# The v of an attention batch's ninth block in a tile of its own

## The chip, the cores and the metric

One core of a Trainium2 chip runs the whole kernel. The metric is the device time of one execution in microseconds (us), the median of three runs. A profile of one further execution shows what each engine did: PE is TensorE (the matrix engine, PEld its weight loads), DVE is VectorE, ACT is ScalarE, POOL is GpSimd, and SP is SyncE, which here only issues DMAs. SPq is SP's queue of such issues.

## The reference, cut to what matters

Inputs `q`, `k`, `v` have shape (4 batches, 8 heads, 576 positions, 64). Three blocks follow one another:

```python
# 1. attention with a window of 64
scores = q @ k.T / 8, masked to 0 <= pos_q - pos_k < 64
attn = softmax(scores)
x = (attn @ v)            # -> (4, 576, 512) after the heads are joined
# 2. Fourier mixing and an MLP
u = x + real(fft over positions and channels)
x = u + relu(layernorm(u) @ w_ch1) @ w_ch2      # 512 -> 2048 -> 512
# 3. a spatially gated MLP
h = gelu(x @ w_in); u, v = halves of h
out = x + (u * (w_sg @ layernorm(v) + b_sg)) @ w_out
```

The change touches only the loading of the attention's `v`.

## The kernel before

Each batch of 576 positions is cut into nine blocks of 64 (`NB = 9`), so attention walks over 36 blocks, numbered n = 9b + j. A block's keys and values are the 128 positions that end with its own 64. For each block the function `attention` does `scores(n)` (eight TensorE matmuls on L328, then on VectorE the masked minimum on L333, then on ScalarE the exponential on L335), `transposes(n)` (L342, copied out by ScalarE on L344), and then, for two blocks at a time, `pv` (L355: 32 products of 65 columns, written to the PSUM tile `pv`, of which there is one buffer). The ninth block, j = 8, has no partner: its `pv` has 16 products. `norm` divides by the row sums on VectorE (L370, L371 and L374); its last instruction, L374, is the last reader of the PSUM tile. `xt` transposes the result (L384), and the folds on L464 to L474 begin the Fourier stage.

The loop runs over steps n = 0 to 38. In step n it emits scores(n), then `load_attn(n + 4)`, then transposes(n - 1), then pv(n - 2) where a pair or a ninth block is complete, then xt(n - 3). `drive` puts pieces of other work between these: the Fourier stage and layernorm of finished batches, and the decoding of weights, which loads 256 KB pieces (`dec_s`, L162) through the same SP queue.

What is loaded when: `load_q` brings q for two blocks in two DMAs (L284, a ring of `QB = 3` tiles), `load_k` brings k for three blocks (L273, three buffers), `load_v` brings v for two blocks in one DMA of 520 KB (L301), and for the ninth block in one of 260 KB (L296). All of v goes through one ring of `VB = 3` tiles of 2 x 520 floats per partition; the ninth block takes a whole one of these and fills half of it. With `VL = 2`, the load for block (b, j) is emitted in step 9b + j - 2, and the pair's pv in step 9b + j + 3.

The order on each engine is not the order of the program text. The kernel is built with `schedule_with_timeline_sim=True` (L1529): at build time a planner simulates the engines and picks, on each engine, the next instruction among those that are ready in the simulation, by priority, which without further marks is the order in which they were emitted. That order is then fixed; each engine works through its list and waits where something is missing. A load into a ring tile is ready when the tile's last reader is done.

Of the kernel before, what the change touches and what calls it, by code (L numbers as in the profile page):

```python
# [11 lines left out]
F32 = mybir.dt.float32  # L12
# [9 lines left out]
NB = S // 64  # L22
# [91 lines left out]
class Kernel:  # L114
# [172 lines left out]

    def load_v(self, b, j):

        w = min(2, NB - j)  # L290
        t = self.ap_.tile([128, 2, 520], F32, tag="v", bufs=VB, name="v")
        v = self.aps["v"][b]
        for i in range(w):
            self.vt[b, j + i] = t[:, i]
        if w == 1:
            self.nc.sync.dma_start(t[:, 0], v[64 * j:64 * j + 128, :])  # L296
        else:
            src = v[64 * j:64 * j + 128, :]
            ap = [list(x) for x in src.ap]
            src = bass.AP(tensor=src.tensor, offset=src.offset, ap=[ap[0], [64 * 520, 2], ap[1]])  # L300
            self.nc.sync.dma_start(t, src)  # L301

    def load_attn(self, n):
        if n < B * NB:
            b, j = divmod(n, NB)
            if n < 2:
                self.load_q(b, j, 1)
            elif j % 2 == 0:
                self.load_q(b, j, min(2, NB - j))
            if j % 3 == 0:  # L310
                self.load_k(b, j // 3)
        if VL <= n < B * NB + VL:
            b, j = divmod(n - VL, NB)
            if j % 2 == 0:
                self.load_v(b, j)

    def attention(self):
# [1218 lines left out]
```

## Time and profile before

| what | value |
|---|---|
| median of 3 runs | 765.17 us (764.11 to 766.25) |
| the profiled execution: its own time | 765.43 us |
| the profiled execution: span from first to last instruction | 763.6 us, mean granted TensorE clock 0.998 |
| TensorE busy | 746.0 us of the span |
| v loads | 16 of 520 KB, 4 of 260 KB |

The span is 1.83 us shorter than the profiled execution's own time. [...]

### The profile page before, as it was taken

The numbers are of one execution on the slowest core, as the hardware profiler recorded it, in microseconds if no ns is written. First come the engines' busy times: TensorE is split into PE (matmuls) and PEld (weight loads), VectorE is DVE, ScalarE is ACT, GpSimd is POOL, SyncE is SP. The second block draws the span as 40 slices with busy tenths as digits, with TensorE's granted clock in tenths as the row PEclk, the third lists the DMA queues.
The fourth block names the chain that finished last, engine by engine and source line by source line (L and its number), as shares of the span: only waits on it lengthen the run. The fifth ranks groups of instructions, "written<-read, shape, count | busy, mean of one in ns | idle before, by whom it ended". The sixth has DMA issues, their size and how long they took to land.

```text
span 763.6 us, 13934 instructions
## 1 busy us (share of the span) xinstructions
PE 746.0 (98%) x4994; PEld 720.1 (94%) x4994; DVE 526.7 (69%) x1482; ACT 350.9 (46%) x837; POOL 192.6 (25%) x244
## 2 busy tenths in 40 slices
PE   7999899899999999999999999999999999999998
PEld 6798798899999999999999999999999898999897
DVE  4768857983446599874588658546987679674662
ACT  5896996745144566331245224124646454231220
POOL 2344464434214450065321112021102211010100
PEclk9999999999999999999999999999999999999999
DMA  9998761433016888584838914753111141114023
GB/s 267 320 298 258 202 209 43 140 110 125 1 30 215 281 262 292 190 330 161 319 118 318 355 59 151 289 207 124 57 58 32 40 132 33 63 32 135 11 73 124
DMA packets 84773, 123.37 MB, mean 162 GB/s; under 512 B 24416, under 2 KB 61664, under 8 KB 84704
## 3 DMA queue, kind: packets, MB, share of 16 engines
q1 hardware_dynamic: 82912, 119.13, 47.0%
q0 software_dynamic: 576, 2.97, 1.0%
q8 instruction: 39, 0.64, 0.3%
q10 hardware_dynamic: 1216, 0.39, 0.2%
q14 instruction: 30, 0.25, 0.1%
HBM read 91.79 MB, written 30.67 MB: 160 GB/s over the span
## 4 chain that ended last, share of the span: by engine, by line
PE 77%; DVE 3%; DMA 1%; issue 1%; ACT 0%; ACTq 0%
PE w L130 7%; PE w L132 7%; PE w L131 7%; PE c L132 6%; PE c L131 6%; PE c L130 6%; PE g L130 6%; PE g L132 6%; PE g L131 5%; PE acc L131 3%; PE acc L132 3%; PE h L130 3%; PE h L131 3%; PE h L132 3%; PE acc L130 3%; DMA dec_s<-in_wo 1%
## 5 line engine op out<-in xcount | busy, mean ns | idle before, releaser
L171 ACT ACTIVATE set<-dec_w 128x256 fp32r<-128x256 f32 x111 | 45.0, 414 | 68.8 <-PE w L131 31.1
L846 POOL TENSOR_TENSOR u<-u 128x384 f32<-128x384 f32 x15 | 18.6, 1243 | 184.8 <-ACT u L845 126.4
L619 POOL TENSOR_TENSOR rq<-rq,mhalf 128x1 f32<-128x1 f32 (+1 forms) x24 | 16.0, 665 | 150.8 <-DVE rq L618 149.7
L335 ACT ACTIVATE s<-s,mx 128x128 f32<-128x128 f32 x144 | 47.5, 393 | 13.3 <-DVE mx L333 13.2
L172 DVE TENSOR_TENSOR set<-dec_w,set 128x256 fp32r<-128x256 f32 x99 | 45.4, 467 | 9.7 <-ACT set L171 3.6
L333 DVE CUSTOM_DVE_ANT_0 s<-sc,mask 128x128 f32<-128x128 f32 x144 | 33.3, 284 | 24.7 <-PE sc L328 13.2
L165 ACT ACTIVATE dec_g<-dec_s 128x256 f32<-128x256 f32 x88 | 37.5, 428 | 27.4 <-DMA dec_s<-in_wi 11.5
L132 PE MATMUL acc<-rh,set 128*128 128x384 f32 x144 | 48.6, 338 | 0.0
L131 PE MATMUL acc<-rl,set 128*128 128x384 f32 x144 | 48.5, 337 | 0.0
L130 PE MATMUL acc<-rh,set 128*128 128x384 f32 x144 | 46.7, 337 | 0.0
L167 DVE SCALAR_TENSOR_TENSOR dec_w<-dec_g,dec_w 128x256 int32<-128x256 int32 x88 | 42.0, 480 | 3.2 <-ACT dec_g L165 2.9
L328 PE MATMUL sc<-k,q 128*128 128x128 f32 x288 | 40.2, 287 | 3.2 <-DVE mx L333 1.8
L846 DVE TENSOR_TENSOR u<-w,u 128x384 f32<-128x384 f32 x44 | 24.3, 552 | 27.4 <-POOL u L846 22.6
L328 PEld LDWEIGHTS sc<-k,q 128*128 128x128 f32 x288 | 35.8, 197 | 5.1 <-issue 1.8
L893 DVE TENSOR_TENSOR uT<-g,uT 128x384 f32<-128x384 f32 x36 | 19.3, 553 | 28.1 <-PE g L132 28.1
L130 PE MATMUL c<-set,set 128*128 128x320 f32 (+2 forms) x120 | 36.2, 303 | 0.0
L132 PE MATMUL c<-set,set 128*128 128x320 f32 (+2 forms) x120 | 36.0, 303 | 0.0
L718 DVE SCALAR_TENSOR_TENSOR rl<-h,rh 128x384 fp32r<-128x384 f32 x36 | 19.8, 551 | 23.3 <-ACT rh L717 23.3
L131 PE MATMUL c<-set,set 128*128 128x320 f32 (+2 forms) x117 | 35.1, 302 | 0.0
L166 DVE TENSOR_SCALAR dec_w<-dec_s 128x256 int32<-128x256 int32 x88 | 31.0, 361 | 5.0 <-DMA dec_s<-in_wo 3.5
L355 PEld LDWEIGHTS pv<-v,pts 128*64 128x64 f32 x576 | 23.3, 139 | 8.0 <-issue 6.4
L845 ACT ACTIVATE u<-w 128x384 f32<-128x384 f32 x29 | 14.1, 487 | 35.9 <-PE w L132 35.0
(383 smaller groups left out, 2603.2 us busy)
## 6 DMA issues: line engine op xcount, KB each, us to landing
dec_s<-in_w SPq DMA_DIRECT2D x64, 256.0 KB, 3.2
v<-in_v SPq DMA_DIRECT2D x16, 520.0 KB, 5.1
xht<-xb SPq DMA_DIRECT2D x10, 768.0 KB, 8.3
xhm<-xb SPq DMA_DIRECT2D x10, 768.0 KB, 7.6
xlm<-xb SPq DMA_DIRECT2D x8, 768.0 KB, 8.2
k<-in_k SPq DMA_DIRECT2D x11, 512.0 KB, 6.3
xf<-u SPq DMA_DIRECT2D x18, 256.0 KB, 3.1
p<-xf SPq DMA_DIRECT2D x24, 192.0 KB, 3.8
```

The source lines that it names most:

```text
L130: mm(out, lhsT=lh, rhs=rh, start=first and i == 0, stop=False)
L131: mm(out, lhsT=lh, rhs=rl, start=False, stop=False)
L132: mm(out, lhsT=ll, rhs=rh, start=False, stop=last and i == n - 1)
L165: nc.scalar.activation(out=g, in_=s[:, :, 1].bitcast(F32), func=AF.Prelu, scale=2.0 ** -112, alpha=-2.0 ** 32)
L166: nc.vector.tensor_scalar(out=w, in0=s[:, :, 0], scalar1=29, scalar2=None, op0=ALU.logical_shift_right)
L167: nc.vector.scalar_tensor_tensor(out=w, in0=g[:].bitcast(I32), scalar=3, in1=w, op0=ALU.logical_shift_left, op1=ALU.bitwise_or)
L171: self.nc.scalar.activation(out=hi, in_=f, func=AF.Copy)
L172: self.low.tensor_tensor(out=lo, in0=f, in1=hi, op=ALU.subtract)
L328: nc.tensor.matmul(sc[:, hp], lhsT=q[:, hp].rearrange("p a b -> p (a b)"), rhs=k[:, hp, o:o + 128], start=True, stop=True)
L333: nc.vector.tensor_tensor_reduce(out=s[:, hp], in0=sc[:, hp], in1=mask, scale=-0.125, scalar=1e30, op0=ALU.add, op1=ALU.min, accum_out=mx[ ...
L335: nc.scalar.activation(out=s[:, hp], in_=s[:, hp], func=AF.Exp, bias=mx[:, hp:hp + 1], scale=-1.0)
L846: add = lambda eng, o, i, j: eng.tensor_tensor(out=o, in0=i, in1=j, op=ALU.add)
```

## The change

The ninth block's v gets a tile of its own under the tag `vlast` (520 floats per partition, one buffer). It is fetched right behind the pair of blocks 6 and 7, in the same call of `load_v`. So its load moves from step 9b + 6 to step 9b + 4 of the loop. The ring of three tiles holds pairs alone: four tiles a batch pass through it instead of five. The number of DMAs, their sizes and sources stay as they were, as do all matmuls. The attention's memory pool grows by 2,080 bytes per partition.

```diff
     def load_v(self, b, j):
-        w = min(2, NB - j)
         t = self.ap_.tile([128, 2, 520], F32, tag="v", bufs=VB, name="v")
         v = self.aps["v"][b]
-        for i in range(w):
+        for i in range(2):
             self.vt[b, j + i] = t[:, i]
-        if w == 1:
-            self.nc.sync.dma_start(t[:, 0], v[64 * j:64 * j + 128, :])
-        else:
-            src = v[64 * j:64 * j + 128, :]
-            ap = [list(x) for x in src.ap]
-            src = bass.AP(tensor=src.tensor, offset=src.offset, ap=[ap[0], [64 * 520, 2], ap[1]])
-            self.nc.sync.dma_start(t, src)
+        src = v[64 * j:64 * j + 128, :]
+        ap = [list(x) for x in src.ap]
+        src = bass.AP(tensor=src.tensor, offset=src.offset, ap=[ap[0], [64 * 520, 2], ap[1]])
+        self.nc.sync.dma_start(t, src)
+        if j == NB - 3:
+            last = self.vt[b, NB - 1] = self.ap_.tile([128, 520], F32, tag="vlast", name="vlast")
+            self.nc.sync.dma_start(last, v[64 * NB - 64:64 * NB + 64, :])
 ...
-            if j % 2 == 0:
+            if j % 2 == 0 and j < NB - 1:
                 self.load_v(b, j)
```

## Rows read from the trace of the kernel before

**Rows 1.** The page: busy us, share of the span and instructions of each engine.
```profile
PE 746.0 (98%) x4994; PEld 720.1 (94%) x4994; DVE 526.7 (69%) x1482; ACT 350.9 (46%) x837; POOL 192.6 (25%) x244
```

**Rows 2.** TensorE's waits over the whole span: us in total, times, longest.
```profile
PE pv L355 <- issue: 2.1, 1, 2.1
...
PE sc L328 <- DMA k<-in_k: 1.3, 2, 1.2
```

**Rows 3.** Windows: length, busy us of each engine, PEclk, DMA share, GB/s.
```profile
20.00:40.00 20.00, 18.47 (x218) 16.08 (x217) 15.73 (x90) 16.50 (x47) 7.52 (x15) 1.00 1.04 327
40.00:60.00 20.00, 19.70 (x227) 18.05 (x227) 13.58 (x78) 18.25 (x58) 8.75 (x17) 1.00 0.97 289
60.00:80.00 20.00, 19.36 (x210) 17.88 (x209) 18.11 (x80) 14.06 (x41) 8.97 (x14) 1.00 0.86 249
80.00:100.00 20.00, 17.14 (x193) 15.31 (x192) 15.46 (x74) 19.44 (x51) 9.32 (x15) 0.91 0.68 184
100.00:120.00 20.00, 20.00 (x233) 18.17 (x231) 12.65 (x69) 17.79 (x51) 13.05 (x19) 1.00 0.56 179
...
140.00:763.60 623.60, 616.64 (x3637) 603.64 (x3637) 426.34 (x1004) 241.71 (x543) 131.66 (x134) 1.00 0.43 148
```

**Rows 4.** Waits of SP's own queue, 60 to 120 us.
```profile
SPq L301 <- PE pv L355: 12.8, 7, 2.8
SPq L506 <- DVE uT L568: 10.2, 2, 10.0
SPq L296 <- PE pv L355: 7.7, 1, 7.7
```

**Rows 5.** Timeline of SP's queue, 17 to 35 us: start, us, issue.
```profile
17.26 0.38 SPq L301 DMA_DIRECT2D v<-in_v  x1
17.84 2.90 SPq L284 DMA_DIRECT2D q<-in_q  x2
...
22.82 1.18 SPq L296 DMA_DIRECT2D v<-in_v  x1
24.10 5.24 SPq L284 DMA_DIRECT2D q<-in_q  x4
...
32.90 0.57 SPq L301 DMA_DIRECT2D v<-in_v  x1
...
34.55 0.44 SPq L301 DMA_DIRECT2D v<-in_v  x1
```

**Rows 6.** Issue to landing: q issued at 20.1, two q from 24.1, v at 34.55.
```profile
DMA to landing us min/median/max: 8.2/8.2/8.2
...
DMA to landing us min/median/max: 9.1/9.3/9.5
...
DMA to landing us min/median/max: 9.7/9.7/9.7
```

**Rows 7.** Timeline of TensorE, 30 to 46 us.
```profile
30.50 2.05 PE L328 MATMUL sc<-k,q 128*128 128x128 f32 x16
...
34.57 1.95 PE L328 MATMUL sc<-k,q 128*128 128x128 f32 x16
...
40.59 1.15 PE L355 MATMUL pv<-v,pts 128*64 128x65 f32 x32
...
44.54 0.33 PE L355 MATMUL pv<-v,pts 128*64 128x65 f32 x2
```

**Rows 8.** Timeline of TensorE around 85 us, with the idle time before.
```profile
85.23 0.30 PE L355 MATMUL pv<-v,pts 128*64 128x65 f32 x2 [2.09 <-issue]
```

**Rows 9.** Timeline of VectorE, 82 to 85 us.
```profile
82.06 1.16 DVE L166 TENSOR_SCALAR dec_w<-dec_s 128x256 int32<-128x256 int32 x1
...
84.45 0.68 DVE L374 TENSOR_TENSOR x<-pv,rd 128x512 f32<-128x512 f32 x1
```

**Rows 10.** Window behind that wait, columns as in Rows 3.
```profile
86.00:88.00 2.00, 2.00 (x11) 1.92 (x10) 1.61 (x7) 1.88 (x7) 1.08 (x3) 0.50 0.49 167
```

**Rows 11.** Groups by line on VectorE, 17 to 108 us: busy us, mean ns.
```profile
L166 DVE TENSOR_SCALAR dec_w<-dec_s 128x256 int32<-128x256 int32 x12 | 4.9, 431 | 0.0
```

## The prediction

> **What bounds the kernel now.** I read first the busy shares, then TensorE's waits, then the windows of the attention stage, then the queue on which v is loaded, and last the few microseconds where TensorE does stand still. TensorE is busy for 746.0 of 763.6 us [rows 1]; the reader is to see that only 17.6 us of idleness exist in the whole kernel. The change touches the attention, which ends near 130 us. From 140 us on TensorE is idle for 623.6 - 616.6 = 7.0 us in 624 [rows 3], and nothing of v is left there. Between 20 and 120 us, where the changed loads lie, the windows give idleness of 1.53, 0.30, 0.64, 2.86 and 0.00 us, together 5.3 us. The window from 80 to 100 us also has a mean granted clock of 0.91: 20 x 0.09 = 1.8 us of full-speed work are lost there. So what the change can win by straightening this stage is at most 5.3 + 1.8 = 7.1 us, 0.9% of the time, and only if it removes every stall there.
>
> Does TensorE wait for v? The list of its waits has only one DMA, k, with 1.3 us, and no v [rows 2]. Its longest wait in the stretch is put down to "issue", 2.1 us before a pv [rows 2, 8]. The code says what that is: pv's PSUM tile has one buffer, and its last reader on VectorE, L374, ran from 84.45 to 85.13; the pv started at 85.23 [rows 8, 9]. That wait is for VectorE, not for v.
>
> Who does wait for v's ring is SP: seven v pairs waited 12.8 us and one ninth block 7.7 us for a pv to free a ring tile [rows 4]. This is the wait that the change attacks. It is a wait of a queue that runs ahead of the engines.
>
> **The change part by part.** *The ring.* Before, a load waits for the reader of the third load before it, and every fifth load is a ninth block. After, the ninth blocks don't count. Batch b+1's first three pairs then wait for batch b's pairs 2, 4 and 6 in place of 4, 6 and the ninth, so each may go one pv earlier; the fourth waits for the first, as before. Queued behind a waiting v load are q, k and weight pieces, and TensorE waits for none of these after the start [rows 2]. I cost the shorter waits at 0: their cover is that v is early already. Where it is least early, v issued at 34.55 lands after 9.7 us, at 44.25, and its pv starts at 44.54 [rows 5 to 7]: 0.3 us to spare, which grows when this load goes earlier. So a gain by landing alone is not to be had, as no pv waits for one.
>
> *The ninth block's load* moves in the first batch from 22.82 to right behind the pair at 17.26, past the two q loads at 17.84 [rows 5]. Its 260 KB at the 327 GB/s that this stretch reached [rows 3] are 0.8 us more in front of those q loads. The second of them starts no later than 20.74 and lands 8.2 us later [rows 5, 6], at 28.9 at most; TensorE needs it for the scores at 30.50 [rows 7]. 28.9 + 0.8 = 29.7: hidden, with 0.8 us left. That slack is the cover; without it the price is 0.8 us once. In the later batches DMA is less full (shares 0.86, 0.68 and 0.56 against 1.04) [rows 3], so I take 0 there too. [...]
>
> *The first pair of the second batch* becomes ready earlier: it needs the pv of the first batch's pair 2 and not pair 4. It was issued at 32.90, behind four q and a k [rows 5]. It can now come before the four q at 24.10, or behind the first two of them. Bound above: 520 KB at 327 GB/s are 1.6 us. The first q pair from 24.10 lands after 9.1 to 9.5 us, at some 33.8; the scores that need it start at 34.57 [rows 5 to 7], 0.8 us later. So a v put in front costs TensorE up to 1.6 - 0.8 = 0.8 us, and one put behind costs nothing. In the order of emission the q pair comes first, so I take 0 and keep 0.8 for the range.
>
> *The order on TensorE.* The planner sees v earlier, so it may put a pv earlier. The pv of the second batch's first pair is emitted in step 12 of the loop, but ran at 40.59, behind the scores of blocks 13 and 14 [rows 7] (scores come in eights, and the two sixteens there are blocks 9 to 12). A pv placed earlier gives TensorE work in its small holes; all idleness from 20 to 60 us is 1.83 us [rows 3], which bounds this gain from above, and 0 from below. I take 0.4, about a fifth, since the holes I can name there come from VectorE and ScalarE too.
>
> *Sum.* Ring 0, ninth block 0, q order 0, pv order -0.4: the profiled execution's 765.43 us become 765.0. That execution lies 0.26 above the median of the three runs, so for a median I say **764.8 us**, the same as before within 0.3% (2.3 us, about what a measurement of this kernel can tell from no change).
>
> **The rivals.** What speaks against "no change" is that the order on all engines is made at build time from simulated times, and v's readiness is one of its inputs. A pv moved by one place moves VectorE's and ScalarE's lists too. [...]
>
> *Faster: the stall at 83 us goes.* Ring waits of up to 2.8 us lie on SP in the same stretch [rows 4], so the lists around it will be remade. L374 came late because VectorE first did weight decoding (L166, 1.16 us where the mean is 0.43) and three masked minima [rows 9, 11]. If L374 comes first, or the pv behind other TensorE work, 3.9 us are won: 765.17 - 3.9 = 761.3. With the small holes before it (1.8 + 0.6 us) it ends near 759; the bound is 765.17 - 7.1 = 758.1. For it speaks that the change only loosens: no load is ready later than before. Against it: nothing in the stall is v.
>
> *Slower: one more stall of this kind.* Its place is the single pv buffer between L374 and the next pv, in any of 20 pv's. If the planner draws a pv forward, because its v is there, to where VectorE still has decoding and folds ahead of the previous L374, TensorE, which can't pass it, stands. It decides from 2.3 us of idleness, or from 0.5 us if the clock falls as it did at 83 us. A stall like the seen one gives 765.17 + 3.9 = 769.1; with the q load of 0.8 us on top 769.9. [...]
>
> *The change does not do what it says.* If the planner keeps its order, SP only waits less and every engine list stays; the time is 765.2. That falls within "no change".
>
> **How the numbers follow.** No change within 0.3%: 0.42, and it is the likeliest single case, so its sum is the predicted time; its own range is 763 to 767.4. Faster, by a stall removed: 0.34. Slower, by a stall made: 0.24; less than faster because readiness is only loosened. The range goes down to 760.0 (the 83 us stall gone and about 1.3 us of the small holes) and up to 769.5 (one new stall of 3.9 us, with half of the q price), which leaves about 1 in 10 outside on either side.
>
> **What would show it.** Right: on SP, waits of L301 for pv fall from 12.8 us to under half, and the last ninth block no longer waits 7.7 us; its load stands directly behind the fourth pair of its batch; TensorE's busy time stays within 1 us of 746.0, and its waits still name no v. The scores at 30.50 and 34.57 start no later than before relative to the pv in front of them. Wrong: the window 80 to 100 us with a clock of 1.00 and under 1 us of idleness (the faster rival), or another window of the attention with a clock below 0.95 or a new pv wait over 2 us (the slower one). My working fails as a whole if the time moves by more than 2.3 us and the idle time between 20 and 140 us does not account for it: then the order behind 140 us was changed too, which I hold for unlikely.

## The result, and the profile after

The changed kernel takes 769.84 us (median of 7 runs, 768.05 to 773.59); the kernel before takes 765.17 (7 runs). The ratio is 1.006, with a 95% interval of 1.0043 to 1.0076: slower by 0.6%, some 4.7 us, where no change was forecast. The profiled execution has a span of 766.6 us, 3.0 us more than the one before; single executions of one kernel lie up to 3.8 us (before) and 5.5 us (changed) apart, so a trace shows where time goes better than how much in the median.

The place of the loss is plain. Number TensorE's matmuls from 0 and count time from the start of the first, which lies at 2.14 us of the span in both traces. Matmul 120 then starts at the same time in both (17.02 and 17.05 us), matmul 300 starts 3.98 us later than before (36.03 against 32.05), matmul 1,320 starts 3.23 us later and the last one 2.90 us later. So all of it is lost between 19 and 38 us of the span, around the end of the first batch, and nothing is lost after the attention. The windows of the changed kernel (columns as in Rows 3; PEclk is the granted TensorE clock as a share of full speed, the DMA share the mean busy share of the 16 DMA engines):

```profile
20.00:40.00 20.00, 16.60 (x189) 14.25 (x187) 13.18 (x68) 12.98 (x35) 4.54 (x13) 0.91 1.14 293
...
28.00:32.00 4.00, 1.65 (x11) 1.19 (x10) 1.68 (x6) 1.80 (x5) 1.65 (x3) 0.94 1.18 295
32.00:36.00 4.00, 4.00 (x45) 3.55 (x44) 2.45 (x8) 0.88 (x2) 0.50 (x2) 0.63 1.17 282
...
80.00:100.00 20.00, 16.37 (x193) 14.33 (x194) 16.93 (x90) 19.15 (x51) 8.47 (x13) 1.00 0.91 227
```

Against [rows 3], the window from 20 to 40 us has 1.9 us more idleness and a granted clock of 0.91 in place of 1.00, another 1.8 us. The clock fell behind the idleness: TensorE was busy for 1.65 of the 4 us from 28 to 32, and the next 4 us were granted 0.63. The window from 80 to 100 us, where the clock had been 0.91, now has 1.00. Note the last two columns: the DMA engines are busier than before (1.14 against 1.04), and move less (293 against 327 GB/s).

TensorE's timeline there, with the wait that was foretold not to come:

```profile
29.18 0.44 PE L383 MATMUL xt<-ident,x 128*128 128x128 f32 x2 [0.99 <-DVE x L373]
30.98 0.30 PE L354 MATMUL pv<-v,pts 128*64 128x65 f32 x2 [1.36 <-DMA v<-in_v]
...
34.32 2.35 PE L327 MATMUL sc<-k,q 128*128 128x128 f32 x16
```

The pv of the first batch's fourth pair waits 1.36 us for its v, and the scores of blocks 9 and 10 start at 34.32, where they had started at 30.50 [rows 7]. SP's queue ahead of it (start, us, issue):

```profile
14.88 0.60 SPq L300 DMA_DIRECT2D vlast<-in_v  x1
15.53 0.56 SPq L273 DMA_DIRECT2D k<-in_k  x1
16.14 2.18 SPq L162 DMA_DIRECT2D dec_s<-in_w  x2
18.41 0.38 SPq L297 DMA_DIRECT2D v<-in_v  x1
22.43 1.73 SPq L284 DMA_DIRECT2D q<-in_q  x2
...
25.20 1.32 SPq L297 DMA_DIRECT2D v<-in_v  x1
26.62 2.49 SPq L284 DMA_DIRECT2D q<-in_q  x1
```

The first ninth block was not put behind its pair, as the text of the change has it: it waits for no ring tile, so the planner found it ready sooner and put it ahead of a k, two weight pieces and the pair itself. In the other three batches, too, the ninth block's load was issued ahead of its pair (42.01 against 51.86 us in the second). The pair, issued at 18.41 (17.26 before, [rows 5]), took this long to land:

```profile
DMA to landing us min/median/max: 12.4/12.4/12.4
```

It reads like a case of order: 260 KB pushed in front of a pair that was then late. The experiments say otherwise.

What the change was for did happen. SP's waits for pv between 60 and 120 us, 12.8 and 7.7 us in [rows 4], are now:

```profile
SPq L297 <- PE pv L354: 5.8, 2, 3.7
...
SPq L300 <- PE pv L354: 2.9, 2, 2.1
```

Part of that fall is not the change's own. In the changed kernel with q back in its old place (e1 and e9 below, the same order) these waits are 9.0 and 5.5 us in one trace and 5.2 and 5.2 us in the other: the sum falls from 20.5 us to 14.5 and 10.4, and to 8.7 where q's loads are slow.

### The profile page after: what moved, and what is told of

It reads as the page before. It is cut to its first block, busy times and chain, and to the rows that moved or that the text cites. A ratio compares the mean times of both kernels' runs of the same rounds, so it can differ in the third digit from the quotient of the medians.

```text
span 766.6 us, 13933 instructions
## 1 busy us (share of the span) xinstructions
PE 747.5 (98%) x4994; PEld 720.5 (94%) x4994; DVE 528.1 (69%) x1482; ACT 351.6 (46%) x837; POOL 191.1 (25%) x244
## 4 chain that ended last, share of the span: by engine, by line
PE 82%; DVE 5%; DMA 2%; issue 1%; ACT 1%; ACTq 0%; DVEq 0%
PE w L130 7%; PE w L132 7%; PE w L131 7%; PE c L132 6%; PE g L130 6%; PE c L131 6%; PE c L130 6%; PE g L132 6%; PE g L131 6%; PE acc L131 3%; PE acc L132 3%; PE h L130 3%; PE h L132 3%; PE acc L130 3%; PE h L131 3%; PE pv L354 1%
## 5 line engine op out<-in xcount | busy, mean ns | idle before, releaser
L332 DVE CUSTOM_DVE_ANT_0 s<-sc,mask 128x128 f32<-128x128 f32 x144 | 32.9, 283 | 22.7 <-PE sc L327 13.6
L716 ACT ACTIVATE rh<-h 128x384 fp32r<-128x384 f32 x36 | 17.3, 482 | 25.1 <-PE h L132 22.2
```

What stands on the lines that cost most here:

```text
L332: nc.vector.tensor_tensor_reduce(out=s[:, hp], in0=sc[:, hp], in1=mask, scale=-0.125, scalar=1e30, op0=ALU.add, op1=ALU.min, accum_out=mx[ ...
```

## The experiments

Two things differ between the kernels. One is the order that the planner made. The other is where tiles lie: the attention's pool ends at a fixed address, the new tile takes the last 2,080 bytes of it, and all other tiles of the pool move down by that much. In the built programs the three q tiles begin at multiples of 512 bytes before, and 480 bytes past one (32 past a multiple of 64) after; k and the mask of the scores move by as much. Each of q's packets writes 256 bytes of a partition. A padded tile or an unused one moves addresses and leaves every instruction and its order as it was, so the two can be told apart.

A packet is one record of the trace's DMA part, with its queue, its bytes and the time that it took. In these records (the main queue, first 140 us) the 17,408 packets of 256 bytes, all of them q's, took 19.1 ns in the mean before and 26.2 ns after. Shared evenly, an estimate, that is 17,408 x 7.1 ns / 16 = 7.7 us more on each of the 16 DMA engines in the attention. The median packet hardly changed (18 and 19 ns); the slowest tenth went from 20 ns and more to 44 ns and more, and the share that took 40 ns or more from 0.7% to 13.6%. The page gives the main queue's packets, MB and share of the 16 engines' span; before:

```profile
q1 hardware_dynamic: 82912, 119.13, 47.0%
```

and after, with the same packets and bytes:

```profile
q1 hardware_dynamic: 82912, 119.13, 48.4%
```

All experiments were timed against the kernel before, 6 to 12 runs each. The table has the place of q past a multiple of 512 bytes, the mean of q's packets, the median and the ratio.

```
kernel                              order   q at  q ns   median us  ratio (95% interval)
changed kernel                      after   480   26.2   769.84     1.0060 (1.0043 to 1.0076)
e1  its tile padded                 after     0   19.0   765.18     0.9996 (0.9983 to 1.0009)
e9  only q moved back               after     0   19.7   765.48     1.0002 (0.9991 to 1.0014)
e2  before, all tiles moved         before  480   25.5   769.38     1.0046 (1.0032 to 1.0061)
e5  before, only q moved            before  480   25.7   767.34     1.0027 (1.0012 to 1.0042)
e6  before, k, v, others moved      before    0   18.8   765.64     1.0005 (0.9995 to 1.0015)
e3  before, all moved, multiple 64  before  448   24.0   767.64     1.0022 (1.0011 to 1.0033)
e10 before, all moved, multiple 128 before  384   22.2   766.74     1.0021 (1.0008 to 1.0034)
e7  before, all moved, multiple 256 before  256   18.7   765.38     1.0004 (0.9990 to 1.0018)
e8  before, v and a table to 512    before    0   19.3   765.05     0.9999 (0.9985 to 1.0014)
e4  padded, ninth behind its pair   new       0   18.5   767.70     1.0029 (1.0015 to 1.0044)
```

**e1: the tile padded.** The changed kernel with one edit:

```diff
-            last = self.vt[b, NB - 1] = self.ap_.tile([128, 520], F32, tag="vlast", name="vlast")
+            last = self.vt[b, NB - 1] = self.ap_.tile([128, 640], F32, tag="vlast", name="vlast")[:, 0:520]
```

> The changed kernel with the ninth block's tile rounded up from 2,080 to 2,560 bytes per partition. All instructions and their order on every engine are those of the changed kernel; only the addresses of the attention's other tiles move, q and k back to multiples of 512 bytes as before the change. Theory A, place: the changed kernel lost time because its new tile moved q, k and v to addresses 32 bytes past a multiple of 64, where the packets of q (256 bytes) took 24.5 to 29 ns in the mean instead of 18 to 20 ns. It expects 764 to 766.5 us, the main queue's share back at 47.0% (48.4% in the changed kernel), and no wait of pv for v near 30 us. Theory B, order: the loss comes from the new order of the loads (the first ninth block ahead of k, two weight pieces and the pair it was to follow) and of TensorE's work. It expects 769 to 771 us and the same wait near 30 us. If both count, the time lies between, near 767 to 768.

Measured: 0.9996. The loss is gone, with the changed kernel's order untouched, the first ninth block still ahead of its pair, and 480 bytes more of memory in use. Theory B falls for this kernel. Its main queue has 46.5%. The verdict rests on the twelve times and not on its trace: the profiled execution was the slowest of the twelve (767.78 us), and its last matmul starts 2.37 us later than before's. What that trace does show is a long stall in another place:

```profile
88.48 0.30 PE L354 MATMUL pv<-v,pts 128*64 128x65 f32 x2 [2.64 <-DVE x L373]
```

This is the same pv, counted from the first one, that waited 2.09 us for VectorE in the kernel before [rows 8].

**e2: the kernel before, moved.** At the end of the pool's tiles an unused one:

```diff
-            x = p.tile([128, 514], F32, tag="x", bufs=2, name="x")
+            x = p.tile([128, 514], F32, tag="x", bufs=2, name="x"); self.spare = getattr(self, "spare", None) or p.tile([128, 520], F32, name="spare")
```

> The kernel before with an unused tile of 2,080 bytes in the attention's pool, at the place that the ninth block's tile has after the change. All instructions and their order are those of the kernel before; q, k and v lie at the addresses of the changed kernel, 32 bytes past a multiple of 64. Theory A, place: 768.5 to 771 us, q's packets at 24 to 29 ns in the mean, the main queue's share near 48.4%. Theory B, order: 764 to 766.5 us. Both: between.

Measured: 1.0046. The old kernel, in its old order, loses most of what the change lost, and early: its matmul 300 starts 3.81 us later than before, 1.15 us of that lost before matmul 60 (counted as above). Its window and its main queue:

```profile
20.00:40.00 20.00, 16.56 (x202) 14.41 (x202) 13.25 (x71) 14.14 (x40) 5.24 (x12) 1.00 1.13 296
```

```profile
q1 hardware_dynamic: 82912, 119.13, 48.4%
```

TensorE's waits in its first 110 us name the late loads:

```profile
PE sc L328 <- DMA q<-in_q: 2.2, 2, 1.3
...
PE pv L355 <- DMA v<-in_v: 1.7, 1, 1.7
```

**e3, e10, e7: which multiple.** As e2, with the unused tile at 528, 544 and 576 floats in place of 520.

> As the one before, but the unused tile has 2,112 bytes, so q and k lie at a multiple of 64 bytes that is no multiple of 128 or 512. If theory A holds and what counts is the multiple of 64: 764 to 766.5 us and q's packets at 18 to 20 ns. If a larger multiple counts: 768.5 to 771 us. Theory B: 764 to 766.5 us.

> The kernel before with an unused tile of 2,176 bytes: q at 384 past a multiple of 512, so every packet of q straddles a multiple of 256, though it begins at a multiple of 128. If a multiple of 256 is needed: 767 to 769 us and q's packets at 24 ns or more, as with 64. If 128 is enough: 764.5 to 766.5 us.

> The kernel before with an unused tile of 2,304 bytes: q and k lie 256 past a multiple of 512, so no packet of q straddles a multiple of 256 (at 448 past a multiple of 512, with 767.64 us, each did). If straddling a multiple of 256 is what slows q's packets: 18 to 20 ns and 764.5 to 766.5 us. If q must lie at a multiple of 512: 24 ns or more and 767 us or more.

Measured: 1.0022, 1.0021 and 1.0004. With q at a multiple of 64 or of 128 that is none of 256, q's packets are slow (24.0 and 22.2 ns) and the time is 0.2% up; at a multiple of 256 both are as before. A packet of 256 bytes that begins at such a multiple never straddles one; at 384, 448 or 480 each does. That a multiple of 64 or of 128 would be enough is refuted. The size was forecast too high: where a larger multiple counts, at least 768.5 us (e3) and 767 us with 24 ns (e10) were expected, and 767.64, and 766.74 with 22.2 ns, came.

**e5, e6: q alone, or all but q.** In e5 an unused tile between q and k moves q and the mask alone; e6 moves k, v and the rest and leaves those two in place, with e2's edit and a tile of 480 bytes (120 floats) at the line below, which is shown as in e5.

```diff
-        self.kt, self.vt = {}, {}
+        self.kt, self.vt = {}, {}; self.gap = p.tile([128, 520], F32, name="gap")
```

> The kernel before with an unused tile of 2,080 bytes between q and k: q (and the mask) lie 32 bytes past a multiple of 64, k and v as before. Order of all instructions as before. Theory Q, it is q's packets of 256 bytes: most of the loss, 768 to 770 us, q's packets at 24 to 29 ns. Theory KV, it is the long packets of k and v (1,024 and 2,080 bytes): 764.5 to 767 us.

> The kernel before with unused tiles that move k, v and the rest 32 bytes past a multiple of 64 and leave q at a multiple of 512. Order as before. Theory Q: 764.5 to 767 us, q's packets at 18 to 20 ns. Theory KV: 768 to 770 us.

Measured: 1.0027 and 1.0005. The place of k and v costs nothing that can be measured; that of q costs 0.3%. The mask moves together with q in both, but what reads the two is no slower: TensorE's products of q and k took 287 ns in the mean before and in the changed kernel, VectorE's masked minima 284 and 283 ns (first 130 us). So it is the loading that costs. e5 came out below its expected 768 us. In it the packets of k, whose place had not moved, took 60.4 ns in the mean (54.6 before), and a q load issued between 10 and 60 us landed after 8.6 us (6.9 before): slow packets of q went here with slower packets of k, which pass through the same queue. Whether the rest up to e2's 1.0046 is an interplay of q's place with that of k and v is open; the intervals overlap.

**e9: q alone moved back, in the changed kernel.** The same line with 120 floats (480 bytes), in the changed kernel.

> The changed kernel with an unused tile of 480 bytes between q and k, which moves q (and the mask) alone back to multiples of 512 bytes; k, v and the ninth block's tile stay where the change put them, and all instructions and their order are those of the changed kernel. Theory Q, q's place alone: 764.5 to 767 us, q's packets at 18 to 20 ns, the main queue's share at 47% or less. If k's and v's place counts too: 767 to 769 us.

Measured: 1.0002. With k, v and the new tile where the change put them, moving q by 480 bytes gives the whole loss back. The same window as above now reads

```profile
20.00:40.00 20.00, 17.28 (x210) 15.09 (x209) 15.69 (x85) 15.82 (x45) 7.13 (x15) 1.00 1.09 329
```

and the main queue

```profile
q1 hardware_dynamic: 82912, 119.13, 47.1%
```

In TensorE's first 110 us no wait for v is left, and that for q is small. The longest of its waits that remain is one of the scores for VectorE, 1.9 us in this execution:

```profile
PE sc L327 <- DVE E L468: 1.9, 1, 1.9
...
PE sc L327 <- DMA q<-in_q: 0.2, 1, 0.2
```

**e8: more of the same, before the change.** Each block of v at a multiple of 512 bytes, and the Fourier table too:

```diff
-        t = self.ap_.tile([128, 2, 520], F32, tag="v", bufs=VB, name="v")
+        t = self.ap_.tile([128, 2, 640], F32, tag="v", bufs=VB, name="v")[:, :, 0:520]
...
-        self.eo, self.fp, self.gr = {}, {}, {}
+        self.eo, self.fp, self.gr = {}, {}, {}; p.tile([128, 88], F32, name="gap0")
```

An unused tile of 192 bytes, made as in e2, keeps q and k at multiples of 512.

> The kernel before with more places at multiples of 512 bytes: each block of v at a stride of 2,560 bytes in its tile (before: 2,080), the first v tile, q and k as before, and the table of the Fourier stage moved by 352 bytes. Order as before. If the long packets of v and of the table lose time by their place: 762 to 764.5 us, v's packets under 95 ns. If only q's short packets count: 764.5 to 766.5 us.

Measured: 0.9999. The packets of 2,080 bytes and the table's gained nothing here by their place.

**e4: the load where the prediction had put it.** e1 with the ninth block's load tied behind its pair in SP's order:

```diff
-        self.nc.sync.dma_start(t, src)
+        pair = self.nc.sync.dma_start(t, src)
...
-            self.nc.sync.dma_start(last, v[64 * NB - 64:64 * NB + 64, :])
+            with self.tc.issue_after(pair.ins): self.nc.sync.dma_start(last, v[64 * NB - 64:64 * NB + 64, :])
```

> The changed kernel with the tile rounded up to 2,560 bytes, and the ninth block's load tied behind its pair in SP's order, as the change's text reads; with the first tile of the kind the planner had put it three loads earlier. Theory A: 763 to 766 us, as the padded kernel without the tie or up to 1 us less. Theory B: 764 to 767 us while the padded kernel without the tie stays at 769 to 771, since the first ninth block no longer delays the pair that pv waited for.

Measured: 1.0029, slower than expected by both theories, with q's packets at their fastest (18.5 ns) and 0.28 us ahead of the kernel before at matmul 300. At matmul 1,320 its trace is 1.71 us behind. In the window from 80 to 100 us it has

```profile
80.00:100.00 20.00, 15.37 (x183) 13.33 (x184) 16.45 (x72) 18.23 (x48) 9.56 (x14) 1.00 0.74 210
```

TensorE is idle there for 4.6 us, 2.86 before [rows 3]. That does not explain the loss, for e9, which loses nothing, is nearly as idle there, 4.25 us:

```profile
80.00:100.00 20.00, 15.75 (x187) 13.62 (x186) 16.36 (x76) 18.47 (x48) 8.39 (x13) 1.00 0.74 195
```

The intervals of e4 and e1 don't overlap, so an order can cost 0.3% after all. The tie made the planner change the order on all engines, not only the place of four loads; which of the moved instructions costs the time is open. No version beat the kernel before.

## Why the prediction was wrong

*The sum.* The working lists four parts, ring, ninth block, q order and pv order, and gives none to the 2,080 bytes by which the pool grows. That is the step that failed: the list of what the change moves was not complete, and the place of the tiles stood at nothing without a reason. The growth of the pool was in the description of the change and in no term, no bound and no rival. In its place the runs showed q's packets at 26.2 ns in the mean where they had been at 19.1, with q at 480 past a multiple of 512. The price, by the pairs with equal order, is 4.7 us in the changed kernel (769.84 against 765.18 in e1) and 3.6 in the kernel before (769.38 against 765.79, the median of its runs beside e2).

*The ring at 0.* Right in its price. SP's waits for pv fell, if less with q in place than in the changed kernel, and with q in place the kernel is as fast as before (e1, e9). That the queue waited less gained nothing in them (0.9996 and 1.0002).

*The ninth block at 0, with 0.8 us of slack.* The place was wrong: the load came out ahead of its pair in all four batches, in the first by a k and two weight pieces, since readiness, not the text, sets the order. The price of 0 held in e1. The kernel with the load in the place that I had assumed is the slower one (e4), for a reason that is open. That the q loads would pay the whole 0.8 us was my estimate; no run shows it by itself. The slack was worked out with landings of 8 to 10 us; with q misplaced the pair's landing took 12.4 us, and the pv waited 1.36 us.

*The order of q and of the second batch's first pair.* The pair did come ahead of the four q (25.20 and 26.62), the dearer of my two cases, for which I had kept 0.8 us. e1 has the same order and shows no loss.

*The pv order at -0.4.* Not to be told: 0.4 us are 0.05%, and e1's 0.9996 has an interval 0.26% wide.

*The rivals.* The slower one, at 769.1, has the right size by accident. Its mechanism, a pv held up by VectorE at the one PSUM buffer, is not what the trace shows: a wait for L373 of 0.99 us stands just ahead, but the pv's own wait is for v, by DMA, and it goes when q's tiles move. Its second half, idleness followed by a lower granted clock, did come, in another place: 0.63 from 32 to 36 us. The stall at 83 us that the faster rival wanted removed is the one that did not go: the same pv waits 2.64 us in e1, 1.38 in e9 and 1.63 in e4. In the changed kernel it waits 0.18 us, and the scores behind it wait 1.93 us for VectorE; there the window from 80 to 100 us was granted 1.00, and part of the loss came back. The 3.9 us that both rivals and the range count for one stall are an estimate, 2.1 us of wait [rows 8] and 1.8 us for a clock of 0.91 over 20 us [rows 3], with 0.50 just behind the wait [rows 10]. No run shows this price by itself; in its place the changed kernel, with that wait at 0.18 us, was 3.98 us behind at matmul 300 and 3.23 us at matmul 1,320.

## What to carry to other kernels

A change that adds a tile can move the other tiles of its pool; here it moved them all. Before a difference of some tenths of a per cent is put down to order or waiting, build the new kernel with the tile rounded up so that the other tiles lie again where they lay past a multiple of 512 bytes, and the old one with an unused tile: same instructions, same order, and only the place differs. Look first at the busy share of the DMA engines against the bytes that they move: busier with fewer GB/s (1.14 and 293 against 1.04 and 327 from 20 to 40 us), with packets and bytes unchanged, was the sign here that single packets had become slower.

## What the runs showed of the hardware

q's loads, whose packets write 256 bytes into each partition, were slower where the tile began off a multiple of 256 bytes: 22.2 to 26.2 ns a packet in the mean at 384, 448 and 480 past a multiple of 512, 18.5 to 19.7 ns at 0 and 256. In DRAM all of q's pieces begin at multiples of 256 bytes of their tensor in all kernels, so it is the side in SBUF that differs. Packets of 1,024 and 2,080 bytes showed no such loss from their own place: in e6 those of k took 55.6 ns and those of v 105.1 (54.6 and 107.1 before). In the first 60 us, where the time is lost, the mean share of the DMA engines was 0.99 before and 1.08 in the changed kernel; whether the cost would stay hidden where they have room, no run shows. Most of q's packets were no slower: the median was 18 ns before and 19 ns in the changed kernel, and the mean rose by those that took more than double, 40 ns or more (0.7% before, 13.6% in the changed kernel). Why those and not the others is open, and so is what happens to a packet that straddles a multiple of 256.
